# Attention tiles that keep to one batch, with a leftover tile, 128-token loads of v and a routing scan by 64 tokens

## The chip, the cores and the metric

The kernel runs on one core of a Trainium2 chip. The metric is the device time of the kernel in microseconds; lower is better. Three runs of the kernel before took 714.41, 713.40 and 714.28 us, the median is 714.28 us.

## The reference

Two things are computed one after the other. First, attention within chunks of 64 tokens, for 8 batches of 576 tokens (9 chunks) with 8 heads of 64 numbers. Then a mixture of 8 experts on the rows of 512 numbers that the attention leaves.

```python
# attention: batch 8, heads 8, seq 576, head_dim 64
scores = scale * np.matmul(q_c, k_c.transpose(0, 1, 2, 4, 3))   # each chunk of 64 tokens for itself
scores = scores - np.max(scores, axis=-1, keepdims=True)
attn = np.exp(scores)
attn = attn / (np.sum(attn, axis=-1, keepdims=True) + 1e-09)
out = np.matmul(attn, v_c)
...
# experts: x is [8, 576, 512], 8 experts, 1024 hidden numbers
for b in range(B):
    prev_e = -1
    for s in range(S):
        fresh_e = int(np.argmax(logits[b, s]))
        if s == 0 or local_gate[b, s] < 0.5:
            e = fresh_e
        else:
            e = prev_e if prev_e >= 0 else fresh_e
        prev_e = e
        ...
        h = np.maximum(x[b, s] @ w1[e], 0.0)
        out[b, s] = p[e] * (h @ w2[e])
```

A token either takes its own best expert or keeps the expert of the token before it in the same batch. This carry runs along the 576 tokens of a batch and starts anew with each batch.

## The kernel before

The 4608 tokens of all batches are taken as one row and cut into 18 tiles of 256 tokens. 256 doesn't divide 576: of every nine tiles six lie in one batch, and three (tiles 2, 4 and 6, and again 11, 13 and 15) cross from one batch into the next.

**Loads.** For a tile, q and k are loaded with two tokens on a partition (512 bytes in one piece for each head), so a tile inside one batch is one DMA of 512 KB for q and one for k, over 128 partitions. A tile that crosses is two DMAs each: 32 and 96 partitions, 64 and 64, or 96 and 32 (`load_qk`, L125). v is loaded with a token on a partition, 256 bytes in one piece for each head. Each chunk of 64 tokens is a DMA of its own onto 64 partitions: chunks 0 and 1 of a tile go to partitions 0 to 63, in columns 0 and 1, and chunks 2 and 3 to partitions 64 to 127 (`load_v`, L137). The write of a finished tile (its 256 rows of 512 numbers, 8 logits and a gate) to the DRAM tensor `x_d` is one DMA of 521 KB (L302). All these, and the loads of the expert weights, are issued by the one queue of the sync engine (SP), in the order of the program; each waits for the buffer that it fills, and for the eighth DMA before it to have landed, since eight semaphores go round.

**The attention loop.** In iteration i (1 to 15) TensorE (PE) works on five tiles at once, in an order written out by hand (`PAR["steady"]`): scores `sc` of tile i+1, transposes of the scaled scores of tile i, values `o` of tile i-1 (L242), transposes of the finished rows and the router logits `lg` of tile i-2, and transposes of q and k of tile i+2. SP issues in iteration i: q and k of tile i+5 (three buffers each), v of tile i+1 (two buffers, so it follows the values of tile i-1), and the write of tile i-2. In iterations 6, 8, 10 and 12 a 512 KB piece of the first expert's weights is added, and in 13 and 14 two pieces each. From iteration 13 no q or k is left to load. VectorE (DVE) does the softmax's maxima and subtractions, the normalisation and all of the routing; ScalarE (ACT) copies the transposes out of PSUM and takes the exponent; GpSimd (POOL) puts the heads of q and k side by side.

**Routing.** `route` handles 18 columns of 128 tokens, once for the first nine tiles (its steps hang in the hooks of iterations 10 to 15) and once for the last nine (in the drain). It finds the best expert and the gate (s1), transposes them so that a column's 128 tokens lie along a row (s2), scans each row (s3, L354 and L355), takes each row's last value (s4), scans these 18 ends in one row, beginning with the end of the half before (`eprev`, s5, L364 to L368), sends the carries back (s6, s7), and counts ranks (s8 to s11). `slots` then inverts the ranks to a list of token numbers for each tile of 128 places of the experts (L559 to L572): `gidx` is the row of `x_d` to gather, `sidx` the row of the output to scatter to. It runs three times: for the first three places in iteration 15, for five more in the drain, and for the rest in the expert phase.

**Drain and expert phase.** After iteration 15 a second order (`PAR["drain"]`) mixes the last tiles' attention, the second half's routing and the first three expert tiles. The expert phase follows, one tile of 128 rows after another, each with 48 matmuls of 128x128 by 128x512 and its gather and scatter.

Of the kernel before, what the change touches and what calls it, by code (L numbers as in the profile page):

```python
# [29 lines left out]
DV = D + 2  # L30
TA = 18
EARLY = 3
NTILE = (2 * EARLY + 1 + 2 * (E - 2) + N // HT + 1) // 2
# [32 lines left out]
def tile_attention_then_moe(ctx: ExitStack, tc, q, k, v, wg, wl, w1, w2, out):  # L66
# [46 lines left out]
    vbuf = [pa1.tile([P, 2, H, DV], F32, name=f"v{i}") for i in range(NV)]  # L113

    def load_qk(i, parts=1):
        qt = pe2.tile([P, H, 2 * D], F32, name="qt", tag="qt", bufs=3)
        kt = pe2.tile([P, H, 2 * D], F32, name="kt", tag="kt", bufs=3)
        t0 = 256 * i
        while t0 < 256 * (i + 1):
            b, s0 = t0 // S, t0 % S  # L120
            n = min(S - s0, 256 * (i + 1) - t0)
            p0 = (t0 - 256 * i) // 2
            for h in range(0, H, H // parts):
                for dst, src in ((qt, q), (kt, k)):
                    nc.sync.dma_start(  # L125
                        dst[p0:p0 + n // 2, h:h + H // parts],
                        src[b, h:h + H // parts, s0:s0 + n, :].rearrange("h (p r) d -> p h (r d)", r=2),
                    )
            t0 += n
        return qt, kt  # L130

    def load_v(i):
        vt = vbuf[i % NV]
        for ch in range(4):
            t0 = 256 * i + 64 * ch
            b, s0 = t0 // S, t0 % S
            nc.sync.dma_start(  # L137
                vt[64 * (ch // 2):64 * (ch // 2) + 64, ch % 2, :, 0:D],
                v[b, :, s0:s0 + 64, :].rearrange("h s d -> s h d"),
            )  # L140
        return vt
# [136 lines left out]
    def router(i, xT, xs, fine=False):  # L278
# [18 lines left out]
        def red():  # L297
            Lt = L[:, 2 * i:2 * i + 2, :]
# [3 lines left out]
            nc.sync.dma_start(x_d[256 * i:256 * i + 256, :].rearrange("(c p) n -> p c n", p=P), xs)  # L302

# [11 lines left out]
    nc.gpsimd.memset(cnt, 0.0)  # L315
    eprev = cpool.tile([1, 1], F32, name="eprev")
    nc.gpsimd.memset(eprev, 0.0)

# [6 lines left out]
    def route(t0, t1, rh_eng):  # L325
# [26 lines left out]
        def s3():  # L352
            sc2 = z["sc2"] = bt([T, 2, P], "sc2")
            V.tensor_tensor_scan(sc2[:, 1], z["aT"], zrow[0:T, 0:P], 1.0, ALU.mult, ALU.add)  # L354
            V.tensor_tensor_scan(sc2[:, 0], z["aT"], z["ps"][0:T, P:2 * P], 0.0, ALU.mult, ALU.add)  # L355

        def s4():
            ps = z["ps"] = trp()
            for n in range(2):
                nc.tensor.transpose(ps[0:1, T * n:T * n + T], z["sc2"][:, n, P - 1:P], ident[0:T, 0:T])  # L360

        def s5():
            endp = bt([1, T], "endp")
            V.tensor_copy(endp, z["ps"][0:1, T:2 * T])  # L364
            cin = z["cin"] = bt([1, T + 1], "cin")
            V.tensor_copy(cin[:, 0:1], eprev)
            V.tensor_tensor_scan(cin[:, 1:T + 1], endp, z["ps"][0:1, 0:T], eprev, ALU.mult, ALU.add)
            V.tensor_copy(eprev, cin[:, T:T + 1])  # L368

        def s6():  # L370
            ps = z["ps"] = trp()
            nc.tensor.transpose(ps[0:T, 0:1], z["cin"][:, 0:T], ident[0:1, 0:1])

        def s7():
            cins = bt([T, 1], "cins")
            V.tensor_copy(cins, z["ps"][0:T, 0:1])
            eT = z["eT"] = bt([T, P], "eT")
            V.scalar_tensor_tensor(eT, z["sc2"][:, 1], cins, z["sc2"][:, 0], ALU.mult, ALU.add)

# [135 lines left out]
    for r in range(2):  # L515
        nc.gpsimd.iota(iota_hp[HT * r:HT * r + HT], [[2, NTILE]], base=r, channel_multiplier=0,
                       allow_small_or_imprecise_dtypes=True)
    iota_t = iota([P, NT], [[1, NT]], dt=BF16, name="iota_t")
    iota_e = iota([P, E], [[1, E]], name="iota_e")
# [10 lines left out]
    for b in range(B):  # L530
        t, p = divmod(b * S, P)
        nc.gpsimd.memset(notfirst[p:p + 1, t:t + 1], 0.0)

# [3 lines left out]
    def slots(pool, q0, q1, halves, qs, tags=({}, {}, {})):  # L537
# [16 lines left out]
        def s2():  # L554
# [10 lines left out]
            id1 = pool[1].tile([P, Q], F32, name=f"id1{q0}", bufs=1)  # L565
            V.scalar_tensor_tensor(id1, inv[:, 0], float(P), inv[:, 1], ALU.mult, ALU.add)
            gi = pa1.tile([P, Q], I32, name=f"gidx{q0}")
# [3 lines left out]
            si = pa1.tile([P, Q], I32, name=f"sidx{q0}")  # L571
            V.scalar_tensor_tensor(si, id1, -1.0, pad, ALU.add, ALU.add)  # L572
            for t in range(q0, q1):
# [425 lines left out]
```

## Time and profile before

| what | value |
|---|---|
| median of three runs | 714.28 us |
| time of the profiled execution | 717.28 us |
| its span in the trace | 715.5 us |
| busy PE, DVE, ACT, POOL | 660.4, 360.0, 272.1, 186.7 us |
| granted TensorE clock, mean | 0.975 |
| DMA packets, bytes | 102930, 97.51 MB |
| packets under 512 B | 42672 |

The attention loop fills about the first quarter of the span (to 166 us), the drain runs to about 225 us, and the rest is the expert phase. A view by stretches gives, for each stretch of time, the busy time of each engine with the number of its instructions, the granted clock of PE, the busy share of the DMA engines (over 1 where packets overlap on an engine) and the GB/s that they moved. A view of waits gives who waited for whom, in total microseconds, times, and the longest. In rows of instructions, `o<-v,pT` means that `o` is written from `v` and `pT`.

### The profile page before, as it was taken

How to read it: one execution, taken by the hardware profiler on the slowest of the kernel's cores; microseconds unless marked ns; L12 is line 12 of the kernel's file. 1: busy time of each engine (PE TensorE's matmuls, PEld its weight loads, DVE VectorE, ACT ScalarE, POOL GpSimd, SP SyncE). 2: the span in 40 equal slices, each digit the busy share in tenths (PEclk: the TensorE clock that was granted, in tenths of full speed). 3: DMA queues.
4: the chain of work that ended last, by engine and by line, in shares of the span. 5: the costliest groups of instructions: out<-in, count | busy, mean ns of one | idle time of the engine just before them, and what ended most of it. 6: DMA issues, size and time to landing. Idle time of an engine off the chain costs nothing. (4 is left out here: it accounts for less than half of the span.)

```text
span 715.5 us, 17196 instructions
## 1 busy us (share of the span) xinstructions
PE 660.4 (92%) x5594; PEld 524.7 (73%) x5594; DVE 360.0 (50%) x852; ACT 272.1 (38%) x432; POOL 186.7 (26%) x230
## 2 busy tenths in 40 slices
PE   4799898887999999999999999999999999999971
PEld 4677676665777788678888887788877888678861
DVE  1566556576784585356242553473575333455320
ACT  2566665565422234442222443422454222432210
POOL 3322233354021232223121231331243211232100
PEclk9999989999999999999999999999999999999996
DMA  9999999999713143245111333441276311234100
GB/s 202 218 207 243 237 234 245 255 238 226 233 66 120 50 149 114 95 147 176 34 49 44 90 127 137 150 157 49 84 229 205 117 47 32 76 118 165 41 29 16
DMA packets 102930, 97.51 MB, mean 136 GB/s; under 512 B 42672, under 2 KB 79536, under 8 KB 102768
## 3 DMA queue, kind: packets, MB, share of 16 engines
q1 hardware_dynamic: 96608, 75.70, 42.0%
q0 software_dynamic: 6160, 19.85, 8.6%
q8 instruction: 78, 1.28, 0.8%
q14 instruction: 84, 0.69, 0.3%
HBM read 76.48 MB, written 19.56 MB: 134 GB/s over the span
## 5 line engine op out<-in xcount | busy, mean ns | idle before, releaser
L641 PE MATMUL y<-w2h,hp 128*128 128x512 f32 x608 | 202.2, 403 | 4.3 <-ACTq L899 3.9
L627 PE MATMUL h<-w1h,xp 128*128 128x512 f32 x608 | 178.3, 403 | 0.0
L641 PEld LDWEIGHTS y<-w2h,hp 128*128 128x128 f32 x608 | 114.7, 189 | 31.1 <-issue 4.1
L627 PEld LDWEIGHTS h<-w1h,xp 128*128 128x128 f32 x608 | 111.4, 189 | 23.8 <-ACTq L879 0.2
L641 PE MATMUL y<-w2l,hp 128*128 128x512 f32 x304 | 120.7, 397 | 2.3 <-DVE w2l L869 2.3
L700 POOL DMA_INDIRECT out<-ysb,sidx x38 | 38.2, 1006 | 267.4 <-DVE ysb L699 221.8
L627 PE MATMUL h<-w1l,xp 128*128 128x512 f32 x304 | 95.9, 397 | 0.0
L590 ACT CAST hp<-tr 128x512 fp32r<-128x512 f32 x76 | 41.4, 589 | 99.7 <-PE tr L588 88.1
L591 DVE TENSOR_TENSOR xp<-tr,xp 128x512 fp32r<-128x512 f32 x39 | 27.0, 691 | 87.0 <-ACTq L879 54.0
L641 PEld LDWEIGHTS y<-w2l,hp 128*128 128x128 f32 x304 | 57.6, 189 | 15.3 <-DVE w2l L869 3.0
L699 DVE TENSOR_SCALAR ysb<-y,ppr 128x512 f32<-128x512 f32 x35 | 26.2, 748 | 83.3 <-PE y L641 71.0
L627 PEld LDWEIGHTS h<-w1l,xp 128*128 128x128 f32 x304 | 57.0, 188 | 14.8 <-DVEq L879 0.7
L613 ACT ACTIVATE pex<-pex 128x8 f32<-128x8 f32 x38 | 7.9, 209 | 141.1 <-DVE pex L612 141.1
L591 DVE TENSOR_TENSOR hp<-tr,hp 128x512 fp32r<-128x512 f32 x76 | 49.3, 685 | 19.1 <-ACT hp L590 18.9
L680 ACT ACTIVATE hsb<-h 128x1024 f32<-128x1024 f32 x35 | 35.9, 1027 | 50.2 <-PE h L627 47.3
L594 POOL DMA_INDIRECT xg<-x_d,gidx x36 | 39.0, 1082 | 42.2 <-issue 17.4
L242 PE MATMUL o<-v,pT 64*64 64x65 f32 x1152 | 33.1, 233 | 13.0 <-DMA v<-in_v 9.5
L242 PEld LDWEIGHTS o<-v,pT 64*64 64x64 f32 x1152 | 25.0, 141 | 23.2 <-DMA v<-in_v 12.8
L588 PE MATMUL tr<-ident,hsb 128*128 128x128 f32 x304 | 40.2, 273 | 0.3 <-ACT hsb L680 0.3
L588 PEld LDWEIGHTS tr<-ident,hsb 128*128 128x128 f32 x304 | 35.3, 140 | 6.7 <-ACT w2h L863 1.2
L869 DVE TENSOR_TENSOR w1l<-raw,w1h 128x1024 fp32r<-128x1024 f32 x21 | 35.4, 1711 | 6.5 <-ACT w1h L863 6.5
L156 POOL COPY qr<-qt 128x512 f32<-128x512 f32 x34 | 19.9, 614 | 64.9 <-issue 26.3
(175 smaller groups left out, 841.0 us busy)
## 6 DMA issues: line engine op xcount, KB each, us to landing
raw<-in_moe_w SPq DMA_DIRECT2D x72, 512.0 KB, 5.3
x_d<-xs SPq DMA_DIRECT2D x18, 521.0 KB, 5.9
v<-in_v SPq DMA_DIRECT2D x72, 128.0 KB, 6.2
qt<-in_q SPq DMA_DIRECT2D x11, 512.0 KB, 6.3
kt<-in_k SPq DMA_DIRECT2D x11, 512.0 KB, 8.3
qt<-in_q SPq DMA_DIRECT2D x6, 256.0 KB, 6.6
kt<-in_k SPq DMA_DIRECT2D x6, 256.0 KB, 6.7
qt<-in_q SPq DMA_DIRECT2D x4, 384.0 KB, 6.7
```

The costliest lines, as they stand in the source:

```text
L156: eng.tensor_copy(dst, src)
L242: nc.tensor.matmul(o[64 * cp:64 * cp + 64, cc, DV * h:DV * h + D + 1], pT[64 * cc:64 * cc + 64, 4 * j + h, 64 * cp:64 * cp + 64], vt[64 * ...
L588: nc.tensor.transpose(ps[:, n], src_of(n), ident)
L590: return [tr, lambda: nc.scalar.copy(hi, box["ps"]), lambda: V.tensor_tensor(lo, box["ps"], hi.bitcast(F32), ALU.subtract)]
L591: lambda: V.tensor_tensor(lo, box["ps"], hi.bitcast(F32), ALU.subtract)]
L594: nc.gpsimd.indirect_dma_start(out=dst, out_offset=None, in_=src, in_offset=bass.IndirectOffsetOnAxis(ap=gidx[t].bitcast(U32), axis=0))
L627: nc.tensor.matmul(hs[:, j], xs[a][:, c], W1[w][c][:, 512 * j:512 * j + 512], start=(c == 0 and n == 0), stop=(c == 3 and n == 2))
L641: nc.tensor.matmul(y, hx[f // 4][a][:, f % 4], W2[w][c][:, f % 2, :], start=(f == 0 and n == 0), stop=(f == 7 and n == 2))
L680: nc.scalar.activation(hsb, hs.rearrange("p j f -> p (j f)"), AF.Relu)
L699: either(mix, lambda: V.tensor_scalar(ysb, y, pr, None, ALU.mult), lambda: y_mixed(ysb, y, ym, pr))
L700: nc.gpsimd.indirect_dma_start(out=out, out_offset=bass.IndirectOffsetOnAxis(ap=sidx[t].bitcast(U32), axis=0), in_=ysb, in_offset=None, bo ...
L869: (nc.gpsimd if c == 1 else nc.vector).tensor_tensor(lo[c], raw[c], hi[c].bitcast(F32), ALU.subtract)
```

## The change

A table `place(i)` says which tokens tile i holds. Eight of every nine tiles now hold 256 tokens of one batch, from its position 0 or 256. The fifth of the nine (`LEFT = 4`, so tiles 4 and 13) takes the last chunk, tokens 512 to 575, of each of four batches. The results of a tile go to the columns `L` of its `slot`, so the four batches of a phase keep 16 columns for whole tiles and the last two for the leftover tile.

In scores and values the chunk on partitions 64·cp and column cc is now 2·cp+cc instead of 2·cc+cp. So the tokens on 128 partitions of one column of `v` are 128 that follow each other, and a DMA loads 128 tokens. A leftover tile loads v as four DMAs of 64 tokens and q and k as four DMAs of 32 partitions each, and writes `x_d` with four DMAs of 64 rows.

The routing scans 64 tokens at a time instead of 128, since a column now holds two chunks that are not neighbours. The 2·16 ends are put in the order of tokens for the scan of ends, and the carry of the leftover chunks is taken from it; nothing is carried from one half to the other, as each half holds four whole batches. Token numbers now differ from rows of `x_d`, so `slots` computes `gidx` as the row of `x_d` and then, by a division by nine chunks and two bits, the row of the output.

On SP's queue, the start of the program, before:

```order
L125 DMA qt<-in_q 128x8x128
L125 DMA kt<-in_k 128x8x128
L137 DMA v_119<-in_v 64x8x64 x4
L125 DMA qt<-in_q 32x8x128
L125 DMA kt<-in_k 32x8x128
L125 DMA qt<-in_q 96x8x128
L125 DMA kt<-in_k 96x8x128
L137 DMA v_120<-in_v 64x8x64 x4
```

and with the change:

```order
L131 DMA qt<-in_q 128x8x128
L131 DMA kt<-in_k 128x8x128
L144 DMA v_119<-in_v 128x8x64 x2
L131 DMA qt<-in_q 128x8x128
L131 DMA kt<-in_k 128x8x128
L144 DMA v_120<-in_v 128x8x64 x2
```

These are q and k of tile 1, v of tile 0, q and k of tile 2 and v of tile 1. Four v loads of 64 partitions became two of 128, and tile 2's four pieces became two whole ones.

The four pieces of tile 4 (two of 64 partitions for q, two for k), which stand a little behind on the same queue, became eight of 32 partitions.

On DVE in the drain, the scan of the ends of the second half's rows (`endp` holds the ends, `cin` the carries; `psm` and `pm` belong to the weights of an early expert tile), before:

```order
L615 TENSOR_REDUCE psm<-pex 128x2
L364 COPY endp<-tr 1x18
L366 COPY cin<-eprev 1x1
L367 SCALAR_TENSOR_TENSOR cin<-endp,eprev,tr 1x18
L368 COPY eprev<-cin 1x1
L616 TENSOR_SCALAR pm<-psm 128x1
```

and with the change:

```order
L660 TENSOR_REDUCE psm<-pex 128x2
L386 COPY endp<-tr 1x2x8x2 x2
L390 MEMSET cin 1x1
L391 SCALAR_TENSOR_TENSOR cin<-endp 1x32
L393 COPY cinT<-cin 1x2x16
L395 COPY cinT<-cin 1x2x2
L661 TENSOR_SCALAR pm<-psm 128x1
```

Four instructions became six between `psm` and `pm`, and the scan runs over 32 ends instead of 18.

On DVE in iteration 15, the end of the first `slots` and the softmax of the last tile behind it, before:

```order
L566 SCALAR_TENSOR_TENSOR id_2940<-inv_2937 128x3
L568 TENSOR_SCALAR gidx_2942<-id_2940 128x3
L570 SCALAR_TENSOR_TENSOR pad_2944<-inv_2937,padidx 128x3
L572 SCALAR_TENSOR_TENSOR sidx_2946<-id_2940,pad_2944 128x3
L204 TENSOR_REDUCE mx_3022<-sc 128x8
```

and with the change:

```order
L604 TENSOR_SCALAR gidx_2930<-id_2928 128x3
L606 SCALAR_TENSOR_TENSOR pad_2932<-inv_2925,padidx 128x3
L609 TENSOR_SCALAR bits_2935<-gidx_2930 128x3
L610 TENSOR_SCALAR bits_2935<-bits_2935 128x3
L611 TENSOR_SCALAR bits_2935<-bits_2935 128x3
L612 SCALAR_TENSOR_TENSOR bits_2935<-bits_2935,gidx_2930 128x3
L613 TENSOR_SCALAR bits_2935<-bits_2935 128x3
L614 TENSOR_SCALAR bits_2935<-bits_2935 128x3
L615 TENSOR_TENSOR pad_2932<-bits_2935,pad_2932 128x3
L616 TENSOR_TENSOR pad_2932<-pad_2932,bits_2935 128x3
L617 TENSOR_TENSOR sidx_2934<-gidx_2930,pad_2932 128x3
L212 TENSOR_REDUCE mx_3019<-sc 128x8
```

One instruction became nine between `pad` and the maxima of the softmax.

The diff, cut to its core:

```diff
@@ -29,6 +29,8 @@
+CR = 64
+LEFT = 4
@@ -112,32 +114,38 @@
+    def place(i):
+        ph, j = divmod(i, 9)
+        if j == LEFT:
+            return 9 * ph + 8, [(4 * ph + n, 512, 64) for n in range(4)]
+        j -= j > LEFT
+        return 9 * ph + j, [(4 * ph + j // 2, 256 * (j % 2), 256)]
+
     def load_qk(i, parts=1):
...
-            b, s0 = t0 // S, t0 % S
-            n = min(S - s0, 256 * (i + 1) - t0)
-            p0 = (t0 - 256 * i) // 2
+        p0 = 0
+        for b, s0, n in place(i)[1]:
...
     def load_v(i):
         vt = vbuf[i % NV]
-        for ch in range(4):
-            t0 = 256 * i + 64 * ch
-            b, s0 = t0 // S, t0 % S
-            nc.sync.dma_start(
-                vt[64 * (ch // 2):64 * (ch // 2) + 64, ch % 2, :, 0:D],
-                v[b, :, s0:s0 + 64, :].rearrange("h s d -> s h d"),
-            )
+        t0 = 0
+        for b, s0, n in place(i)[1]:
+            for s1 in range(s0, s0 + n, P):
+                m = min(P, s0 + n - s1)
+                nc.sync.dma_start(
+                    vt[t0 % P:t0 % P + m, t0 // P, :, 0:D],
+                    v[b, :, s1:s1 + m, :].rearrange("h s d -> s h d"),
+                )
+                t0 += m
@@ -188,7 +196,7 @@
-                ch = 2 * cc + cp
+                ch = 2 * cp + cc
@@ -295,11 +303,17 @@
-            nc.sync.dma_start(x_d[256 * i:256 * i + 256, :].rearrange("(c p) n -> p c n", p=P), xs)
+            if len(rows) == 1:
+                (b, s0, n), = rows
+                nc.sync.dma_start(x_d[S * b + s0:S * b + s0 + n, :].rearrange("(c p) n -> p c n", p=P), xs)
+            else:
+                for m, (b, s0, n) in enumerate(rows):
+                    nc.sync.dma_start(x_d[S * b + s0:S * b + s0 + n, :], xs[64 * (m // 2):64 * (m // 2) + 64, m % 2])
@@ -351,31 +363,50 @@
-            V.tensor_tensor_scan(sc2[:, 1], z["aT"], zrow[0:T, 0:P], 1.0, ALU.mult, ALU.add)
-            V.tensor_tensor_scan(sc2[:, 0], z["aT"], z["ps"][0:T, P:2 * P], 0.0, ALU.mult, ALU.add)
+            for cp in range(2):
+                half = slice(64 * cp, 64 * cp + 64)
+                V.tensor_tensor_scan(sc2[:, 1, half], z["aT"][:, half], zrow[0:T, 0:64], 1.0, ALU.mult, ALU.add)
+                V.tensor_tensor_scan(sc2[:, 0, half], z["aT"][:, half], z["ps"][0:T, P + 64 * cp:P + 64 * cp + 64],
+                                     0.0, ALU.mult, ALU.add)
...
-                nc.tensor.transpose(ps[0:1, T * n:T * n + T], z["sc2"][:, n, P - 1:P], ident[0:T, 0:T])
+                for cp in range(2):
+                    nc.tensor.transpose(ps[0:1, T * (2 * n + cp):T * (2 * n + cp) + T],
+                                        sc2_end(n, cp), ident[0:T, 0:T])
...
-            nc.tensor.transpose(ps[0:T, 0:1], z["cin"][:, 0:T], ident[0:1, 0:1])
+            for cp in range(2):
+                nc.tensor.transpose(ps[0:T, cp:cp + 1], z["cinT"][:, cp], ident[0:1, 0:1])
@@ -515,7 +546,12 @@
-    iota_t = iota([P, NT], [[1, NT]], dt=BF16, name="iota_t")
+    iota_t = cpool.tile([P, NT], BF16, name="iota_t")
+    for ph in range(2):
+        iota(None, [[9, 4], [4, 2], [2, 2]], base=36 * ph, dst=iota_t[:, TA * ph:TA * ph + TA - 2])
+        for cp in range(2):
+            iota(None, [[9, 2]], base=36 * ph + 18 * cp + 8 - cp,
+                 dst=iota_t[64 * cp:64 * cp + 64, TA * ph + TA - 2:TA * ph + TA])
@@ -563,13 +599,22 @@
-            V.scalar_tensor_tensor(si, id1, -1.0, pad, ALU.add, ALU.add)
+            bits = pool[1].tile([P, 2, Q], I32, name=f"bits{q0}", bufs=1)
+            V.tensor_single_scalar(bits[:, 0], gi, 6, ALU.logical_shift_right)
+            V.tensor_single_scalar(bits[:, 1], bits[:, 0], 57.0, ALU.mult)
+            V.tensor_single_scalar(bits[:, 0], bits[:, 1], 9, ALU.logical_shift_right)
+            V.scalar_tensor_tensor(bits[:, 1], bits[:, 0], float(-S), gi, ALU.mult, ALU.add)
...
+            V.tensor_tensor(si, gi, pad, ALU.add)
```

More of the change, by code (lines that the diff above doesn't have):

```diff
@@ L128, in load_qk @@
                     )
-            t0 += n
+            p0 += n // 2
         return qt, kt
@@ L297, in red @@
         def red():
-            Lt = L[:, 2 * i:2 * i + 2, :]
+            slot, rows = place(i)
+            Lt = L[:, 2 * slot:2 * slot + 2, :]
             nc.vector.tensor_reduce(
@@ L315, in tile_attention_then_moe @@
     nc.gpsimd.memset(cnt, 0.0)
-    eprev = cpool.tile([1, 1], F32, name="eprev")
-    nc.gpsimd.memset(eprev, 0.0)
     def trp():
@@ L359, in s4 @@
             for n in range(2):
-                nc.tensor.transpose(ps[0:1, T * n:T * n + T], z["sc2"][:, n, P - 1:P], ident[0:T, 0:T])
-        def s5():
[L363 to L368, printed above, removed]
+                for cp in range(2):
+                    nc.tensor.transpose(ps[0:1, T * (2 * n + cp):T * (2 * n + cp) + T],
+                                        sc2_end(n, cp), ident[0:T, 0:T])
@@ new lines, in sc2_end @@
+        def sc2_end(n, cp):
+            return z["sc2"][:, n, 64 * cp + 63:64 * cp + 64]
+        def s5():
+            R = T - 2
+            endp = bt([1, 2, 2 * R], "endp")
+            for n in range(2):
+                V.tensor_copy(endp[:, n].rearrange("a (j p c) -> a p j c", p=2, c=2),
+                              z["ps"][0:1, 2 * T * n:2 * T * n + 2 * T].rearrange("a (p t) -> a p t", p=2)[:, :, 0:R]
+                              .rearrange("a p (j c) -> a p j c", c=2))
+            cin = z["cin"] = bt([1, 2 * R + 1], "cin")
+            V.memset(cin[:, 0:1], 0.0)
+            V.tensor_tensor_scan(cin[:, 1:2 * R + 1], endp[:, 1], endp[:, 0], 0.0, ALU.mult, ALU.add)
+            cinT = z["cinT"] = bt([1, 2, T], "cinT")
+            V.tensor_copy(cinT[:, :, 0:R].rearrange("a p (j c) -> a p j c", c=2),
+                          cin[:, 0:2 * R].rearrange("a (j p c) -> a p j c", p=2, c=2))
+            V.tensor_copy(cinT[:, :, R:T], cin[:, 1:2 * R + 1].rearrange("a (p c n) -> a p c n", p=2, c=2)[:, :, :, 7])
@@ L370, in s6 @@
         def s6():
             ps = z["ps"] = trp()
-            nc.tensor.transpose(ps[0:T, 0:1], z["cin"][:, 0:T], ident[0:1, 0:1])
+            for cp in range(2):
+                nc.tensor.transpose(ps[0:T, cp:cp + 1], z["cinT"][:, cp], ident[0:1, 0:1])
         def s7():
-            cins = bt([T, 1], "cins")
-            V.tensor_copy(cins, z["ps"][0:T, 0:1])
+            cins = bt([T, 2], "cins")
+            V.tensor_copy(cins, z["ps"][0:T, 0:2])
             eT = z["eT"] = bt([T, P], "eT")
-            V.scalar_tensor_tensor(eT, z["sc2"][:, 1], cins, z["sc2"][:, 0], ALU.mult, ALU.add)
+            for cp in range(2):
+                half = slice(64 * cp, 64 * cp + 64)
+                V.scalar_tensor_tensor(eT[:, half], z["sc2"][:, 1, half], cins[:, cp:cp + 1], z["sc2"][:, 0, half],
+                                       ALU.mult, ALU.add)
@@ L517, in tile_attention_then_moe @@
                        allow_small_or_imprecise_dtypes=True)
-    iota_t = iota([P, NT], [[1, NT]], dt=BF16, name="iota_t")
+    iota_t = cpool.tile([P, NT], BF16, name="iota_t")
+    for ph in range(2):
+        iota(None, [[9, 4], [4, 2], [2, 2]], base=36 * ph, dst=iota_t[:, TA * ph:TA * ph + TA - 2])
+        for cp in range(2):
+            iota(None, [[9, 2]], base=36 * ph + 18 * cp + 8 - cp,
+                 dst=iota_t[64 * cp:64 * cp + 64, TA * ph + TA - 2:TA * ph + TA])
     iota_e = iota([P, E], [[1, E]], name="iota_e")
@@ L530, in tile_attention_then_moe @@
     for b in range(B):
-        t, p = divmod(b * S, P)
-        nc.gpsimd.memset(notfirst[p:p + 1, t:t + 1], 0.0)
+        t = TA * (b // 4) + 4 * (b % 4)
+        nc.gpsimd.memset(notfirst[0:1, t:t + 1], 0.0)
     gidx, sidx = {}, {}
@@ L565, in s2 @@
             id1 = pool[1].tile([P, Q], F32, name=f"id1{q0}", bufs=1)
[L566 removed]
+            V.scalar_tensor_tensor(id1, inv[:, 0], float(CR), inv[:, 1], ALU.mult, ALU.add)
             gi = pa1.tile([P, Q], I32, name=f"gidx{q0}")
@@ L571, in s2 @@
             si = pa1.tile([P, Q], I32, name=f"sidx{q0}")
-            V.scalar_tensor_tensor(si, id1, -1.0, pad, ALU.add, ALU.add)
+            bits = pool[1].tile([P, 2, Q], I32, name=f"bits{q0}", bufs=1)
[3 more added lines that the diff above has]
+            V.scalar_tensor_tensor(bits[:, 1], bits[:, 0], float(-S), gi, ALU.mult, ALU.add)
+            V.tensor_single_scalar(bits[:, 0], bits[:, 1], 64, ALU.bitwise_and)
+            V.tensor_scalar(bits[:, 1], bits[:, 1], 1, 64, ALU.logical_shift_right, ALU.bitwise_and)
+            V.tensor_tensor(pad, bits[:, 0], pad, ALU.add)
+            V.tensor_tensor(pad, pad, bits[:, 1], ALU.subtract)
+            V.tensor_tensor(si, gi, pad, ALU.add)
             for t in range(q0, q1):
```

2 lines of the change are left out of this document (removed).

## The prediction

> **What bounds the kernel now.** I read the page's slices first, then who waits for whom, then the attention loop cut into its iterations, and last what the sync engine's queue does in it. The slices of the page:
>
> ```profile
> span 715.5 us, 17196 instructions
> PE   4799898887999999999999999999999999999971
> DMA  9999999999713143245111333441276311234100
> GB/s 202 218 207 243 237 234 245 255 238 226 233 66 120 50 149 114 95 147 176 34 49 44 90 127 137 150 157 49 84 229 205 117 47 32 76 118 165 41 29 16
> ```
>
> A slice is 17.9 us. From the twelfth on PE is at 9 and the DMA engines are mostly idle: the drain and the expert phase are bound by PE, so what shortens the attention loop ahead of them shortens the whole. In the first ten slices, the loop, it is the other way round: DMA at 9 throughout, PE with holes. What PE waits for there, from the view of waits over the whole run:
>
> ```profile
> PEld o L242 <- DMA v<-in_v: 12.8, 19, 1.3
> PE o L242 <- DMA v<-in_v: 9.5, 14, 1.2
> ```
>
> The two rows overlap (a weight load and the matmul behind it). The values wait for v, and for no other load so much. The stretches below run from the first score matmul of one iteration to that of the next (us, then busy us with the number of instructions of PE, PEld, DVE, ACT and POOL, granted clock, DMA share, GB/s); the thirteen from 34.30 to 154.20 are iterations 2 to 14, of which some are shown:
>
> ```profile
> 34.30:42.20 7.90, 7.55 (x174) 6.14 (x173) 5.16 (x13) 5.43 (x10) 3.28 (x6) 1.00 1.21 215
> 51.40:58.70 7.30, 7.30 (x175) 6.00 (x174) 5.23 (x15) 5.56 (x10) 2.34 (x4) 1.00 1.14 256
> ...
> 84.30:97.50 13.20, 10.74 (x171) 8.37 (x170) 5.26 (x14) 5.53 (x10) 2.35 (x4) 0.74 1.17 244
> 97.50:104.80 7.30, 7.30 (x176) 5.98 (x174) 5.24 (x15) 5.91 (x11) 3.62 (x5) 1.00 1.19 227
> ...
> 124.40:137.10 12.70, 9.75 (x174) 7.40 (x173) 6.67 (x21) 6.97 (x13) 3.60 (x5) 0.87 1.15 243
> ...
> 146.90:154.20 7.30, 7.30 (x175) 5.98 (x174) 5.82 (x16) 5.05 (x9) 3.61 (x5) 1.00 1.14 262
> 154.20:166.10 11.90, 8.10 (x189) 6.53 (x188) 10.39 (x38) 8.11 (x14) 8.28 (x13) 1.00 1.13 282
> 180.00:230.00 50.00, 49.14 (x373) 37.20 (x372) 35.77 (x133) 14.25 (x25) 8.04 (x10) 1.00 0.47 150
> ```
>
> An iteration in which PE never waits takes 7.30 us. The thirteen take 154.2 - 34.3 = 119.9 us, and 13 x 7.3 would be 94.9: 25.0 us are waits, and the DMA share is above 1 in long and short iterations alike. So the DMA stream is the bound, and 25.0 us is the most that it can give back in these iterations before PE binds. The queue itself (start, duration of the issue):
>
> ```profile
> 59.77 0.76 SPq L125 DMA_DIRECT2D qt<-in_q  x1
> 60.64 0.85 SPq L125 DMA_DIRECT2D kt<-in_k  x1
> 61.59 4.36 SPq L137 DMA_DIRECT2D v<-in_v  x4
> 66.05 1.27 SPq L302 DMA_DIRECT2D x_d<-xs  x1
> 67.41 1.18 SPq L125 DMA_DIRECT2D qt<-in_q  x1
> ...
> 172.36 2.65 SPq L137 DMA_DIRECT2D v<-in_v  x4
> ```
>
> SP issues without a pause: four v issues take 4.36 us here, 2.65 us at 172.36, where nothing stands in the way. It is held up by the transfers.
>
> **How fast each kind of transfer goes.** Loads arrive some time after their issue, so I cut stretches in which one kind is most of what moves:
>
> ```profile
> 63.00:65.00 2.00, 2.00 (x22) 1.42 (x21) 1.28 (x3) 1.17 (x3) 1.14 (x2) 1.00 1.09 318
> 66.00:69.00 3.00, 3.00 (x81) 2.77 (x82) 2.02 (x7) 2.22 (x5) 0.62 (x2) 1.00 1.37 161
> 81.00:83.00 2.00, 2.00 (x48) 1.42 (x40) 1.02 (x2) 1.58 (x4) 1.58 (x3) 1.00 1.19 215
> 100.00:103.00 3.00, 3.00 (x53) 2.19 (x48) 2.55 (x7) 2.26 (x5) 2.28 (x3) 1.00 1.22 208
> 174.00:177.00 3.00, 3.00 (x31) 2.35 (x35) 0.69 (x1) 2.11 (x4) 0.00 (x0) 0.58 0.77 173
> ```
>
> 63 to 65 is q and k of a whole tile, on 128 partitions: 318 GB/s. 81 to 83 is tile 11, in pieces of 32 and 96 partitions (215), and 100 to 103 tile 13, in pieces of 64 (208). Same bytes, same 512-byte packets, two thirds of the rate: a DMA on half of the partitions goes slower. 66 to 69 is v, on 64 partitions, with 256-byte packets: 161. 174 to 177 is v too, but alone: 173 GB/s at a DMA share of 0.77. So the engines can move v with less busy time than they need in the loop, where 161 GB/s cost a share of 1.37: packets there hold an engine while they wait for something that engines share. If it is the same that slows half-wide q and k, v on 128 partitions is free of it.
>
> [...]
>
> **The terms.** *v.* A tile's v is 4 x 128 KB = 0.524 MB; at 161 GB/s 3.26 us. On 128 partitions the row of v alone gives 173 / 0.77 = 225 GB/s at a share of 1.0: 2.33 us. Bounds: 161 still (the packets' own size is the limit; no gain, and nothing gives a loss, since packets and bytes stay the same), or 318 as for whole q and k: 1.65 us. I take 225, for it is v's own row: 0.93 us a tile. The last load on which the loop depends in this way is v of tile 13 (iterations 13 and 14 have no q or k to load). Whole tiles up to there: 0 to 12 without the leftover tile 4, that is 12, and 12 x 0.93 = 11.2 us.
>
> *q and k.* Tiles 2, 6, 11 and 15 were split 32 and 96: 1.049 MB at 215 GB/s 4.9 us, whole at 318 3.3: 4 x 1.6 = 6.4 us. Tiles 4 and 13 stay narrow (32 instead of 64 partitions; the row at 215 holds pieces of 32 as well and isn't slower than 208): 0.
>
> *The leftover tile's write.* 0.53 MB of tile 4 from 64 partitions at a time: at 208 GB/s 2.5 us against 1.7 at 318, so +0.8. Tile 13's comes in iteration 15, when there is room.
>
> So the stream is 11.2 + 6.4 - 0.8 = 16.8 us ahead when v of tile 13 lands. That is less than the 25.0 us, so PE can follow.
>
> What is added to the engines, from their rows:
>
> ```profile
> 12.75 1.97 PE L164 MATMUL tr<-ident,qr 128*128 128x128 f32 x8 [0.84 <-POOL qr L156]
> L572 DVE SCALAR_TENSOR_TENSOR sidx<-id,pad 128x3 int32<-128x3 f32 (+2 forms) x3 | 0.5, 176 | 0.1
> L354 DVE TENSOR_TENSOR_SCAN sc<-aT,zrow 18x128 f32<-18x128 f32 x2 | 0.8, 408 | 0.2 <-ACT aT L350 0.2
> L367 DVE TENSOR_TENSOR_SCAN cin<-endp,eprev,tr 1x18 f32<-1x18 f32 x2 | 0.5, 238 | 0.0
> L360 PE MATMUL tr<-ident,sc 18*1 18x18 f32 x4 | 0.4, 179 | 0.0
> L516 POOL IOTA iota_hp<- 64x46 bf16 x2 | 0.3, 168 | 0.1
> ```
>
> *Slots:* eight more small DVE instructions each time, 8 x 0.176 = 1.4 us. The first time they stand in iteration 15 ahead of the last softmax, where DVE is busy for 10.39 of 11.90 us: +1.4. In the drain and the expert phase PE has other work in front of it (49.14 of 50.00 us busy): 0, and up to 1.4 each without that cover. What matters early, `gidx`, is written before them as it was, so no gather is late.
>
> *Routing:* a half needs two more scans (64 long, by the rows for 128 and 18 about 0.31 us each: 4 x 0.31 instead of 2 x 0.40, +0.44), two more copies on the ends and one more product: about +0.9 us on DVE, in iterations 10 to 13 beside PE's work, in the drain under it; 0, and 0.9 each without cover. PE gets three more small transposes a half, 3 x 0.18 = 0.5 us; the first half's fall into waits, the second half's come on top: +0.5.
>
> *Start:* five more iotas on POOL, 5 x 0.168 less one memset = 0.7 us, ahead of the heads of tile 1, for which PE already waits 0.84 us. The stream, not the start, decides when iteration 14 can go on, so 0; 0.7 if I am wrong there.
>
> SP has 26 issues fewer (32 of v fewer, 6 of `x_d` more); as it is held up by transfers, 0.
>
> Sum: -16.8 + 1.4 + 0.5 = -14.9 us. The profiled execution took 717.28 us (span 715.5), so it would be 702.4 there; the median of the runs, 714.28, is 3.0 lower, and becomes 699.4.
>
> **The rivals.** *v stays slow.* If 161 GB/s is what 256-byte packets give, only the q and k term is left: 14.9 - 11.2 = 3.7, 710.6 us. For it: v is slower than half-wide q and k (161 against 208). Against it: the same packets at 173 with a share of 0.77. [...]
>
> *v at the full rate.* 318 GB/s would save 1.6 instead of 0.93 us a tile, 8 us more in 12 tiles: 24.8 us, nearly all of the 25.0; with 1.9 us of added work a gain of 22.9, 691.4 us. PE's 7.30 us an iteration would be the bound, and waits for v would be gone. Against it: v's share of 0.77 at 173.
>
> *Slower.* The serial chains on DVE come to decide: `slots` in front of the last softmax, the routing of the second half in front of the gathers. Price, if nothing covers them: 3 x 1.4 + 2 x 0.9 + 2 x 0.5 + 0.7 = 7.7 us. It decides from the point where the stream gives less than that, so with v as slow as before: 714.3 - 5.6 + 7.7 = 716.4 us. Against it: PE is at 49.14 of 50 us in the drain, so the chains lie under it.
>
> **How the numbers follow.** The forecast, v between about 195 and 265 GB/s and the end between 696 and 704, has 0.58; v slow, 0.18; v at the full rate, 0.18; slower, 0.06. The likeliest time is 699.4 us. The range goes to both bounds of v: 691 to 710.5, with 0.8 inside, since the slow cases reach beyond it. About 0.2% (1.4 us) is what a measurement of this kernel can tell from no change. All cases but the last are faster by more; a part of the slow-v case could lose its rest to the chains: faster 0.90, same 0.04, slower 0.06.
>
> **What would show it.** Stretches in which v alone moves go from 161 to about 225 GB/s, with a DMA share nearer to 1. The waits of `o` for v fall from 12.8 and 9.5 us to under 5. Iterations without a weight load come to 7.3 to 7.6 us; those with one, and those that load or write a leftover tile, stay longer. The last iteration keeps its length of about 12 us or grows by 1.4. The expert phase keeps its length. It is wrong if v's rate stays under 180 GB/s, if the loop shortens and the drain grows by as much, or if PE waits for q and k of the leftover tiles.

## The result and the profile after

| | kernel before | changed kernel |
|---|---|---|
| median, first comparison (4 and 4 runs) | 714.35 us | 702.80 us (702.37 to 703.45) |
| median, second comparison (17 and 6 runs) | 715.11 us | 700.66 us (696.55 to 705.85) |
| profiled execution, its span | 717.28, 715.5 us | 702.94, 700.9 us |

The first comparison gives a ratio of 0.9836, 95% interval 0.9813 to 0.9858; the second 0.9813, 0.9773 to 0.9852. So the change saves 11.7 and 13.4 us by the ratios. The forecast was 699.4 us in a range of 691 to 710.5, and 702.4 us for the profiled execution. Single runs spread more than the first four show: the ten runs of the changed kernel lie between 696.6 and 705.9 us.

The slices of the page, each 17.5 us now:

```profile
span 700.9 us, 17188 instructions
PE   3789898979999999999999999999999999999971
DMA  8999999977531145314111542350466211225100
GB/s 240 257 236 264 260 250 298 281 205 203 162 110 44 48 154 180 100 67 167 63 34 47 158 136 83 123 178 32 128 208 241 87 33 47 79 105 168 49 22 15
```

PE reaches its unbroken row of 9 about one slice earlier than before. The waits of PE and of its weight loads over the whole run, in microseconds, count and longest:

```profile
PE sc L201 <- issue: 7.0, 3, 3.0
PE o L250 <- issue: 1.2, 3, 0.6
PE o L250 <- DMA v<-in_v: 0.9, 1, 0.9
PEld o L250 <- DMA v<-in_v: 1.4, 2, 1.0
```

The waits of `o` for v, 12.8 and 9.5 us before, are 1.4 and 0.9. But a row that was small stands at the top: PE stands still inside score blocks for 7.0 us in three places and waits for nothing that the profile shows ("issue"). The iterations from one first score matmul to the next, with busy PE, PEld, DVE, ACT and POOL, granted clock, DMA share and GB/s:

```profile
33.20:40.40 7.20, 7.20 (x171) 5.94 (x170) 5.04 (x12) 5.42 (x10) 2.35 (x4) 1.00 0.99 261
40.40:47.80 7.40, 7.40 (x175) 6.09 (x174) 5.16 (x15) 5.50 (x10) 2.35 (x4) 1.00 1.04 274
47.80:58.60 10.80, 8.95 (x171) 7.30 (x170) 5.33 (x15) 5.49 (x10) 2.35 (x4) 0.84 0.75 210
...
73.30:83.00 9.70, 7.58 (x175) 6.15 (x174) 5.19 (x15) 5.46 (x10) 2.35 (x4) 1.00 0.95 233
83.00:90.20 7.20, 7.20 (x173) 5.92 (x172) 5.13 (x15) 5.42 (x10) 2.35 (x4) 1.00 1.06 283
...
112.50:122.60 10.10, 7.97 (x178) 6.40 (x176) 6.90 (x25) 7.29 (x13) 3.62 (x5) 1.00 1.10 300
...
139.30:153.20 13.90, 9.67 (x189) 7.89 (x188) 9.54 (x38) 7.88 (x14) 8.31 (x13) 0.88 0.77 216
```

The last score block of the loop starts at 153.2 us instead of 166.1. Undisturbed iterations are at 7.20 us. Those of 10.8, 9.7 and 13.9 us hold the three stalls (1.85, 2.12 and 3.03 us); that of 10.1 us holds the 0.9 us for v and a wait of 1.2 us for the routing. Stretches with mostly v, and the last with q and k:

```profile
41.00:43.00 2.00, 2.00 (x74) 1.77 (x68) 1.34 (x3) 1.86 (x4) 0.00 (x0) 1.00 1.11 262
66.50:68.50 2.00, 2.00 (x65) 1.65 (x59) 1.43 (x3) 1.86 (x4) 0.00 (x0) 1.00 1.15 273
85.00:87.00 2.00, 2.00 (x50) 1.57 (x48) 1.96 (x5) 1.43 (x4) 0.08 (x1) 1.00 1.03 238
46.00:47.50 1.50, 1.50 (x41) 1.43 (x42) 0.68 (x3) 0.84 (x3) 1.17 (x2) 1.00 1.13 337
```

v runs at 238 to 273 GB/s with a DMA share of 1.03 to 1.15, against 161 at 1.37 before. After the loop little changed: from the first expert matmul to PE's last it was 521.6 us before (179.3 to 700.9) and is 521.3 now (165.0 to 686.3).

### The profile page after: what moved, and what is told of

Its sections match the earlier page's. It is cut to its first block, busy times and chain, and to the rows that moved or that the text cites. A ratio compares the mean times of both kernels' runs of the same rounds, so it can differ in the third digit from the quotient of the medians.

```text
span 700.9 us, 17188 instructions
## 1 busy us (share of the span) xinstructions
PE 650.8 (93%) x5600; PEld 519.6 (74%) x5600; DVE 362.4 (52%) x886; ACT 272.1 (39%) x432; POOL 186.5 (27%) x234
## 5 line engine op out<-in xcount | busy, mean ns | idle before, releaser
L914 DVE TENSOR_TENSOR w2l<-raw,w2h 128x1024 fp32r<-128x1024 f32 x21 | 36.5, 1787 | 0.0
L908 ACT CAST w2h<-raw 128x1024 fp32r<-128x1024 f32 x28 | 28.5, 1048 | 17.9 <-PE y L686 13.1
L212 DVE TENSOR_REDUCE mx<-sc 128x8 f32<-128x512 f32 x36 | 23.2, 686 | 22.2 <-PE sc L201 22.2
```

Of the source, the lines that this page charges most:

```text
L212: nc.vector.tensor_reduce(mxs[a], sc.rearrange("p j h c k -> p (j h c) k")[:, a:b], AX.X, ALU.max)
L908: nc.scalar.copy(hi[c], raw[c])
L914: (nc.gpsimd if c == 1 else nc.vector).tensor_tensor(lo[c], raw[c], hi[c].bitcast(F32), ALU.subtract)
```

## The experiments

All times are medians, and ratios are against the kernel before on the same chip. The table takes three numbers from each kernel's profile: the start of the last score block of the loop, the PEld waits of `o` for v, and PE's own stalls (the rows `sc`, `o`, `tr` <- issue together). The text below takes the kernels in groups. The rows with "other tokens" and "left out" compute something else, which their sections name. Two more kernels that leave loads out stand in the text alone.

| kernel | us | ratio, interval | last block | for v | stalls |
|---|---|---|---|---|---|
| before | 714.35 | | 166.1 | 12.8 | 3.5 |
| changed, first | 702.80 | 0.9836, 0.9813 to 0.9858 | 153.2 | 1.4 | 8.7 |
| changed, again | 700.66 | 0.9813, 0.9773 to 0.9852 | 149.7 | 0.4 | 5.4 |
| changed, v on 64, in turn | 702.34 | 0.9826, 0.9787 to 0.9865 | 157.2 | 2.6 | 7.9 |
| changed, v on 64, low first | 705.28 | 0.9873, 0.9843 to 0.9904 | 155.3 | 5.9 | 3.5 |
| changed, v by half the heads | 697.05 | 0.9754, 0.9709 to 0.9799 | 152.8 | 3.0 | 6.1 |
| the same again | 700.91 | 0.9802, 0.9766 to 0.9839 | 155.8 | 3.3 | 9.2 |
| changed, q and k cut | 699.49 | 0.9781, 0.9734 to 0.9827 | 152.3 | 1.4 | 7.6 |
| changed, both undone | 706.61 | 0.9895, 0.9855 to 0.9934 | 156.3 | 10.3 | 1.1 |
| before, v halves in turn | 713.23 | 0.9971, 0.9948 to 0.9994 | 164.1 | 12.6 | 4.4 |
| before, q and k whole (other tokens) | 711.00 | 0.9916, 0.9890 to 0.9941 | 162.1 | 6.8 | 7.2 |
| changed, `bits` left out | 704.99 | 0.9855, 0.9814 to 0.9895 | 161.2 | 8.3 | 6.5 |

### Is it the width of v?

First, v of whole tiles on 64 partitions again, as four transfers in place of two:

```diff
-                nc.sync.dma_start(vt[t0 % P:t0 % P + m, t0 // P, :, 0:D], v[b, :, s1:s1 + m, :]...)
+                for u in range(0, m, 64):
+                    nc.sync.dma_start(vt[t0 % P + u:t0 % P + u + 64, t0 // P, :, 0:D], v[b, :, s1 + u:s1 + u + 64, :]...)
```

> The changed kernel, but v of each whole tile comes as four transfers of 64 partitions and 128 KB again, instead of two of 128 partitions. Theory (it is the width of the transfer in partitions that limits v): v alone moves at 161 to 180 GB/s again, the waits of o for v come back, and the time is what the prediction had for slow v, 709 to 713 us. Rival (the gain came from elsewhere: the order of the tiles, fewer pieces of q and k): 703 to 705 us.

Measured: 702.34 us, no loss. And v was slow in it; a stretch with nothing but v:

```profile
61.00:63.00 2.00, 2.00 (x46) 1.76 (x45) 2.00 (x4) 1.39 (x3) 0.00 (x0) 1.00 0.55 120
```

120 GB/s at a DMA share of 0.55: the engines are not full, PE is busy throughout, and a slow v costs nothing here. Second, the same count and size of transfers on all 128 partitions:

```diff
+                for h in range(0, H, 64 * H // m):
+                    nc.sync.dma_start(vt[..., h:h + 64 * H // m, 0:D], v[b, h:h + 64 * H // m, s1:s1 + m, :]...)
```

> The changed kernel, but v of each whole tile comes as four transfers of 128 KB, each of all 128 partitions and half of the heads. Count and size of the transfers are those of the kernel with 64 partitions, only the width differs. Theory (width): like the changed kernel, 702 to 704 us, v at about 250 GB/s. Rival (number and size of the transfers): like the kernel with v on 64 partitions, 709 to 713 us.

Measured: 697.05 us. By its interval that would be better than the changed kernel, so both were run again on one chip.

> The changed kernel once more, on the same chip as the next three, so that they can be set against it: 700 to 704 us if the chip is like the first.

> The changed kernel with v by halves of the heads, four transfers of 128 partitions a tile, once more beside the changed kernel. If its 697.05 us was a matter of the chip, it and the changed kernel agree within 2 us; if smaller transfers on all partitions are better, it stays 3 to 6 us ahead.

Measured: 700.66 and 700.91 us. The lead of the 697 did not come back; whether it was chance or the other chip is open. Number and size of the transfers make no difference that these runs resolve. The two profiles of the changed kernel differ by 3.5 us at the last score block (153.2 and 149.7), and by 3.3 us in PE's stalls (8.7 and 5.4): the stalls vary between executions of one kernel.

The first experiment had put the halves in turn: low, high, low, high. The kernel before issues low, low, high, high. So the same narrow transfers in that order:

```diff
-            for s1 in range(s0, s0 + n, P):
-                m = min(P, s0 + n - s1)
+            for s1, m in ((s0 + u, 64) for u in ((0, 128, 64, 192) if n == 256 else (0,))):
```

> The changed kernel with v of whole tiles on 64 partitions, like the run that cost nothing, but in the order in which the kernel before issues them: both transfers of partitions 0 to 63 first, then both of 64 to 127 (there: 0 to 63 and 64 to 127 in turn). Theory (two transfers that follow each other onto the same half of the partitions slow each other; halves in turn fill both): the loop gets back most of the 9 us that the run with halves in turn still saved, 708 to 713 us, v's packets take about 65 us of all 16 engines as before instead of 53. Rival (the gain lies in the order of the tiles and the leftover tiles, not in v): 701 to 704 us.

Measured: 705.28 us, 4.6 more than the changed kernel on the same chip, between the two expectations. The intervals of the two ratios overlap (0.9843 to 0.9904, 0.9773 to 0.9852), so the loss is near the edge of what the runs resolve. Its profile, first two stretches of v, then the waits:

```profile
37.00:40.00 3.00, 3.00 (x56) 2.24 (x55) 2.08 (x6) 2.02 (x4) 1.55 (x3) 1.00 1.17 158
77.00:80.00 3.00, 3.00 (x57) 2.19 (x55) 1.82 (x6) 2.29 (x4) 1.79 (x4) 1.00 1.04 177
```

```profile
PE o L250 <- DMA v<-in_v: 5.1, 5, 2.3
PEld o L250 <- DMA v<-in_v: 5.9, 5, 2.4
```

v is back at 158 to 177 GB/s: its rate does follow the width. But only 5.9 us of the waits for v come back, not 12.8. A rate that falls by a third costs far less here than before the change.

### Is it the pieces of q and k?

In the changed kernel, q and k of tiles 2, 6, 11 and 15 in pieces of 32 and 96 partitions:

```diff
+        if i in (2, 6, 11, 15):
+            (b, s0, n), = rows
+            rows = [(b, s0, 64), (b, s0 + 64, 192)]
```

> The changed kernel, but q and k of tiles 2, 6, 11 and 15 come in pieces of 32 and 96 partitions again. The prediction put 6.4 us on these four. Theory A (the stream still bounds the loop): 708 to 709.5 us. Theory B (with v faster SP now pauses for buffers, so the stream has room for 1.6 us in three of four such tiles): 702.5 to 705 us.

Measured: 699.49 us, below the range of either theory and no loss, so B is the nearer. Then this edit and the narrow v, low first, together:

> The changed kernel with both widths undone at once: v of whole tiles on 64 partitions, low half first, and q and k of tiles 2, 6, 11 and 15 in pieces of 32 and 96 partitions. Alone, the first cost 4.6 us and the second nothing. Theory (the stream has slack for one of them, not for both): 709 to 714 us, the last score block of the loop (iteration 17) starts at 162 to 166 us instead of 150 to 153. Rival (each width counts by itself, and the rest of the gain lies in the order of the tiles and in the two leftover tiles): 704 to 707 us, the last score block at 154 to 158 us.

Measured: 706.61 us, last score block at 156.3: the rival. With both widths undone the kernel is still faster than before by 0.9895, that is 7.5 us. So the widths of the transfers are not all of the gain, perhaps not half. What a cut tile does here, tile 11, pieces of 32 and 96 partitions, behind its small piece:

```profile
75.50:77.00 1.50, 1.50 (x17) 1.01 (x16) 1.11 (x2) 1.08 (x3) 1.18 (x2) 1.00 1.09 307
```

307 GB/s on 96 partitions, but only at the end of the burst. The kernel before showed 215 for the same pieces of the same tile; the prediction built its q and k term on that row. Taken whole, tile 11's q and k ran at 261 here (the middle 90% of its 512-byte packets, by their starts); the rows are the kernel before, this kernel, and the changed kernel with the tile uncut:

```profile
79.10:84.20 5.10, 5.03 (x92) 4.05 (x92) 3.38 (x9) 2.97 (x6) 2.34 (x4) 1.00 1.15 214
```

```profile
73.50:77.50 4.00, 3.64 (x78) 2.83 (x80) 2.62 (x7) 2.30 (x5) 1.40 (x3) 1.00 1.06 261
```

```profile
70.70:73.70 3.00, 3.00 (x75) 2.60 (x76) 1.64 (x6) 1.94 (x5) 1.69 (x3) 1.00 1.07 320
```

For all four tiles it is 203 to 218 GB/s before, 236 to 261 here and 299 to 335 uncut. So a cut slows a tile within one batch too, and the tiles that straddle two batches were slower yet.

From the other side, the kernel before with each part alone. The halves of v in turn:

```diff
-        for ch in range(4):
+        for ch in (0, 2, 1, 3):
```

> The kernel before, with one thing changed: the four transfers of v of a tile go to partitions 0 to 63 and 64 to 127 in turn, instead of twice to the one half and then twice to the other. Theory (halves in turn fill both halves of what the partitions are reached through): 704 to 708 us, a large part of the whole change's gain. Rival (the order within v is worth nothing, the order of the tiles is): 713 to 716 us.

Measured: 713.23 us, 0.9971, so 2.1 us better, with 12.6 us of waits for v still there: the rival. So it is not shown that the partitions are reached through two halves. Then q and k whole; the tiles that straddle two batches read 256 tokens of the first one, so these tiles work on other tokens than the reference's:

```diff
-            n = min(S - s0, 256 * (i + 1) - t0)
+            s0 = min(s0, S - 256)
+            n = 256
```

> The kernel before, with q and k of every tile in one piece of 128 partitions: the six tiles that straddle two batches read 256 tokens of the first of them instead (so these tiles' q and k are other tokens than the reference's). v stays as it was, on 64 partitions, low half first. It measures the pieces of q and k where the stream has no slack; with both widths undone in the changed kernel 8.8 us of the gain were still there. Theory (the pieces of q and k cost here what the prediction put on them, 6.4 us for the four tiles and a little more for the other two): 705 to 709 us, the last score block of the loop at 156 to 160 us. Rival (pieces cost nothing here either; the rest of the gain lies in something else that the tiles within one batch bring): 713 to 716 us, the last score block at 163 to 167 us.

Measured: 711.0 us, 0.9916 (0.9890 to 0.9941), so 6.0 us better (4.2 to 7.9); its last score block is at 162.1, between the two expectations. The waits:

```profile
PEld o L243 <- DMA v<-in_v: 6.8, 10, 1.5
PE o L243 <- DMA v<-in_v: 5.1, 6, 1.4
```

They are nearly halved, though v is loaded as before. q and k of the six tiles arrive in 20.8 us together instead of 29.5 (again the middle 90% of their packets), and 6.0 of these 8.7 us come out as time. But these are six tiles; the prediction had 6.4 us for four of them. If all count alike, four would be worth 4.0 us, an estimate. In the changed kernel, cutting four cost nothing with v on 128 partitions, and with narrow v, between the ratios 0.9873 and 0.9895, 1.6 us that their intervals do not resolve. What differs is that before the pieces came from two batches. Whether that is the cause is open: the leftover tiles' pieces come from four, and they arrive in 3.9 to 5.7 us in nine traces of kernels with the change that load everything, the six tiles before in 4.6 to 5.1. Why those go slower, no run here shows.

### The eight small DVE instructions

The eight `bits` instructions of `slots` left out; rows of the result then stand at other places:

```diff
-            V.tensor_single_scalar(bits[:, 0], gi, 6, ALU.logical_shift_right)
...
-            V.tensor_tensor(pad, pad, bits[:, 1], ALU.subtract)
             V.tensor_tensor(si, gi, pad, ALU.add)
```

> The changed kernel without the eight small DVE instructions of slots that turn an address in the new row order into the reference's row (left out: rows of the result then stand at other places). The prediction put +1.4 us on them in iteration 15, where they stand ahead of the last softmax. Theory A (as predicted): iteration 15 falls from 11.9 to about 10.5 us. Theory B (PE has other work in front of it until that softmax is needed): iteration 15 stays at 11.9 us and the time within 1 us of the changed kernel's.

Measured: 704.99 us, 2.2 and 4.3 us above the changed kernel's medians instead of within 1 us, with intervals that overlap; and iteration 15 keeps its length. DVE is the third group of the first two rows, without `bits` and of the changed kernel's second profile:

```profile
149.20:161.20 12.00, 7.96 (x192) 6.48 (x191) 10.46 (x38) 8.02 (x14) 8.28 (x13) 1.00 0.83 225
```

```profile
137.80:149.70 11.90, 7.88 (x189) 6.45 (x188) 10.39 (x38) 7.98 (x14) 8.27 (x13) 1.00 1.09 301
```

Both have 38 DVE instructions: `bits` do not lie in that iteration at all, but behind it. The changed kernel, DVE behind the last score block, start and duration:

```profile
153.89 0.17 DVE L604 TENSOR_SCALAR gidx<-id 128x3 int32<-128x3 f32 x1
...
154.09 0.17 DVE L609 TENSOR_SCALAR bits<-gidx 128x3 int32<-128x3 int32 x1
...
155.78 0.16 DVE L617 TENSOR_TENSOR sidx<-gidx,pad 128x3 int32<-128x3 int32 x1
155.98 1.29 DVE L212 TENSOR_REDUCE mx<-sc 128x8 f32<-128x512 f32 x2
```

And where they are left out, the same softmax:

```profile
165.41 1.29 DVE L212 TENSOR_REDUCE mx<-sc 128x8 f32<-128x512 f32 x2 [3.13 <-PE tr L172]
```

DVE waits 3.13 us for PE there, and the softmax starts 4.23 us after its scores (161.18 to 165.41). With `bits` it starts 2.77 us after them (153.21 to 155.98), right behind the 1.85 us of `bits`. In the kernel before it was 1.38 us (166.14 to 167.52):

```profile
167.52 1.29 DVE L204 TENSOR_REDUCE mx<-sc 128x8 f32<-128x512 f32 x2 [0.27 <-PE sc L193]
```

So `bits` do hold up this softmax by 1.4 us, and leaving them out let another wait hold it up for longer; this run can't price its start. What follows shows no cost: from the last score block to PE's last matmul it is 534.8 us in the kernel before, 533.1 and 530.2 in the changed kernel's two profiles, and 532.7 without `bits`.

This profile also shows something that its edit hardly causes: 8.3 us of waits for v, with v on 128 partitions, all of them ahead of 149 us, where the first `bits` would come behind 162. Its median is 5.8 us below this profiled execution (710.77 us), so single executions can lose the slack again.

### The stalls in the score blocks

v loaded for the first two tiles alone (later tiles use stale values; their loads are left out):

```diff
         vt = vbuf[i % NV]
+        if i > 1:
+            return vt
```

> The changed kernel, but v is loaded for the first two tiles alone, and all later tiles use these values; the loads of v from tile 2 on are left out. Theory A (PE and its own stalls bound the loop now; 2.3 us of waits for v are left): 700 to 703 us. Theory B (the stream still bounds): 690 to 695 us, near the predicted time for v at the full rate or below. The stalls inside the score matmuls for which the profile names nothing (7.0 us in three places) stay as they are if they are PE's own fetching of instructions, and shrink to under 2 us if busy DMA engines hold that fetching up.

The whole took 750.83 us, since stale values send tokens to other experts and one more expert tile is computed (PE's `y` products are 624 instead of 608). The loop can be read: its last score block starts at 145.5 us, 4 to 8 us ahead of the changed kernel's two profiles, and the stalls of `sc` fall from 7.0 (2.9 in the second profile) to 0.2 us. Added to the changed kernel's time that is between the two theories, and near the sum of the stalls. So busy DMA engines have to do with them. To see how, look at the changed kernel around two of them, start, duration, and in brackets the idle time:

```profile
48.18 0.51 PE L201 MATMUL sc<-kT,qT 64*64 64x64 f32 x21
50.55 0.47 PE L201 MATMUL sc<-kT,qT 64*64 64x64 f32 x17 [1.85 <-issue]
```

```profile
73.70 0.51 PE L201 MATMUL sc<-kT,qT 64*64 64x64 f32 x18
76.33 0.46 PE L201 MATMUL sc<-kT,qT 64*64 64x64 f32 x16 [2.12 <-issue]
```

And the DMA queues of the changed kernel in the stretches 45 to 48 and 48 to 49.5 us (packets, MB, share of the engines):

```profile
DMA packets 1876, 0.96 MB, mean 319 GB/s; under 512 B 24, under 2 KB 1871, under 8 KB 1876
...
q1 hardware_dynamic: 1876, 0.96, 107.9%
```

```profile
q1 hardware_dynamic: 899, 0.25, 70.2%
q8 instruction: 1, 0.02, 4.0%
```

In the first, q and k of a tile run at 319 GB/s and nothing else. Right behind them comes one 16 KB packet of the queue that the page calls "instruction" (48.3 to 49.3 us), and PE goes on 1.3 us after its end. At the second stall it is the same (73.9 to 74.8, PE at 76.3, 1.5 us later). So q and k of tiles 8 and 11, which make these two bursts, were left out:

```diff
+        qt, kt = qkbuf[i % 3]
+        if i in (8, 11):
+            return qt, kt
```

> The changed kernel without the loads of q and k of tiles 8 and 11 (left out; these tiles use what is in the buffers). In the changed kernel their transfers fill the DMA engines at 310 to 350 GB/s from 45 to 48 and from 70 to 74 us, a packet of 16 KB of the instruction queue starts right behind each (48.3, 73.9 us), and PE stands still inside a score block until 1.3 to 1.5 us after that packet's end. Theory (the fetch of instructions stands behind the burst): without the two bursts the fetches come 1 to 2 us earlier and the two stalls (1.85 and 2.12 us) are gone or under 0.5 us; stalls elsewhere can stay. Rival (the fetch has its own latency at these places of the program, whatever DMA does): both stalls stay at 1.3 us or more.

Its one run took 697.74 us. The two iterations with these stalls, 10.8 and 9.7 us in the changed kernel:

```profile
46.00:53.90 7.90, 7.42 (x171) 6.02 (x170) 5.17 (x15) 5.46 (x10) 2.35 (x4) 1.00 1.08 232
72.00:79.30 7.30, 7.30 (x175) 6.02 (x174) 5.18 (x15) 5.49 (x10) 2.35 (x4) 1.00 0.82 174
```

0.48 us is left of the first stall, nothing of the second: the theory. But the sum hardly falls. It is 7.0 us, 6.5 of it elsewhere now, one stall behind the burst of tile 10 (59 to 64 us), with the instruction packet at 63.2:

```profile
65.50 0.51 PE L253 MATMUL o<-v,pT 64*64 64x65 f32 x18 [1.79 <-issue]
```

This fits a fetch of PE's instructions that is served only when a burst of q and k lets it through, and counts of PE's records in the traces fit it too. In the fourteen traces 64 stalls of over 0.2 us stand in the loop (from 25 us to the last score block). All lie at places that are 256 of PE's instructions apart, to within one (matmuls, weight loads and semaphore instructions), and in all of them PE goes on 1.2 to 1.9 us after the end of a 16 KB packet. So the places are fixed by the program; what varies is when the packet starts. For the three long stalls of the changed kernel's first profile it starts 5.4, 5.5 and 6.3 us after PE has passed the place before. Without the two bursts it is 3.6 and 4.9 us at the first two, and without the loads of v at most 3.7 us at any place (from 34 us on). An estimate from these numbers: an iteration of 7.2 us has some 350 of PE's instructions, so 256 take 5.3 us; the packet takes 1.0 us, and PE goes on 1.4 us later. A packet that starts over 2.9 us after the passing then makes PE wait. That the packets carry PE's instructions is inferred from these counts and the queue's name. When the fetch is asked for, no view shows; that it queues behind the burst, rather than being asked for late, stays argued.

## Why the prediction was right, and where not

**What bounds, and the sum.** The forecast for the profiled execution, 702.4 us, met 702.94. The stream is what set the loop's pace: the waits for v went as said (under 5 us), the loop is 12.9 us shorter, iterations come to 7.2 us, and the expert phase kept its length. The last step, "the median of the runs is 3.0 lower, and becomes 699.4", failed in the first comparison: the profiled execution of the kernel before lay 3 us above its median by chance, the changed kernel's did not (702.94, median 702.80). An offset between one execution and a median belongs to the execution. That the sum came so near is in part luck: its two large terms are not what the runs found for them, a gain and a loss were not in it, and the second profiled execution took 696.55 us.

**v, 11.2 us.** The rate was right in direction and a little low: 225 forecast, 238 to 273 measured. What v's packets wait for in the loop of the kernel before, and whether the engines share it, no view shows. The step that failed is from the rate to the time, "12 x 0.93". Undoing it costs 4.6 us (low first) or nothing that can be measured (halves in turn). A transfer that is faster by 0.93 us gives 0.93 us only while the stream is behind at that tile; in the changed kernel the stream has room for it.

**q and k, 6.4 us.** The sign held, the size was too high where the prediction stood, at the kernel before: 6.0 us for six tiles, about 4.0 for four. The reason, "a DMA on half of the partitions goes slower", held for v on 64 partitions, low half first (158 to 177 GB/s against 238 to 273 on 128), and in part here: tiles 2, 6, 11 and 15, cut within one batch, run at 236 to 261 GB/s, against 299 to 335 uncut, but the straddling tiles' 203 to 218 had something else in it. And in the changed kernel the cut cost no time that shows.

**The two are not a sum.** By the ratios both undone lose 5.9 us, where 11.2 and 6.4 were forecast; 7.5 us of the gain stay. A part of what stays can be seen in the stream: with both undone q and k of the six tiles that straddled arrive in 24.8 us together, 29.5 before, and v of 13 tiles (0 to 13 without 4) in 39.8, 47.5 before (middle 90% of the packets of each), on the old widths of v and of four of the six. The prediction had booked that under width. How much of the 7.5 us is the straddling of batches and how much the leftover tiles and the new order stays open; no run separates those.

**What took back a part.** "PE can follow" was counted from 25.0 us of waits, and nothing was priced that could take their place. PE's own stalls did: 3.5 us before, 8.7 and 5.4 after. Most rows of the table fit an exchange: with both undone, waits of 10.3 and stalls of 1.1; with q and k cut, 1.4 and 7.6. That without `bits`, 8.3 and 6.5, does not. In the first profile one stall of 1.85 us also came with a granted clock of 0.84 over the iteration, so that this iteration is 3.6 us longer than the 7.2 of its neighbours.

**Slots and routing, +1.4 and +0.5.** The step "the first time they stand in iteration 15" was wrong by its place: they stand behind it. They are ahead of the last softmax, as said, and hold it up by 1.4 us, but that does not reach the end: the time behind the last score block did not grow. Iteration 15 took 11.9 us in the second profile, and 13.9 in the first with a stall of 3.03 us in it. For routing, one wait showed (`tr` for `cinT`, 1.2 us), where PE waited 0.8 us for `cin` in the kernel before. The term of +0.8 us for the leftover tile's write no run prices.

**The rivals.** v did not stay slow, and the DVE chains did not come to decide. v came between the forecast and the full rate; the time of that rival, 691.4, needed PE at 7.3 us throughout, which the stalls forbid.

## What to carry to other kernels

Price a faster transfer by the time for which something waits behind it, not by its own saving times its count: terms that shorten one backlog replace each other, so undo each in the new kernel and do each alone in the old one before a gain is given to a cause. When a wait goes, look what was hidden in it; here PE's own stalls came out from under the waits for v and took back 1.9 to 5.2 of some 12 us. A rate that is read from one stretch belongs to that stretch: 307 GB/s at the end of a burst was 261 over the whole of it. And before "narrow is slow" is concluded from pieces, find the same widths where nothing else differs.

## What the runs showed of the hardware

- PE stops for up to 3.2 us in the middle of a block of ready matmuls, at places that lie 256 of its instructions apart, and goes on 1.2 to 1.9 us after the end of a 16 KB packet of the instruction queue (64 stalls in 14 traces). Where the stall was long in the changed kernel's first profile, the packet started 5.4 to 6.3 us after PE had passed the place before. Without the loads of v from tile 2 on, 1.7 us of such stalls were left; without two bursts the stalls behind them, 1.85 and 2.12 us, were 0.48 us and nothing, and the sum of all was 7.0 us, 6.5 of it elsewhere. Of the 20 such places that PE passed from 26 to 144 us in the changed kernel's first profile, five had a stall, of 0.2 to 3.0 us.
- Stretches of mostly v, in 256-byte packets, ran at 238 to 273 GB/s on 128 partitions and at 158 to 177 on 64, low half first. On 128 partitions the packets' size alone did not hold v to 161.
- q and k of tiles 2, 6, 11 and 15, in 512-byte packets and each of a single batch, ran at 299 to 335 GB/s on 128 partitions and at 236 to 261 in pieces of 32 and 96.
- On one chip the changed kernel's six runs spread over 9.3 us (696.55 to 705.85), the kernel before's 17 over 5.2 us (712.35 to 717.5). Which places stall, and how long, differs between executions: 8.7 us of PE's stalls in the changed kernel's first profile, 5.4 in its second.
